# Window attention into a mixture of attention experts: fp16 pairs scaled by the largest v, stage 1 in two head pairs in step, and a new order of all engines

## The chip, the cores and the metric

The kernel runs on one core of one Trainium2 chip. The metric is the device time of one execution in microseconds, and the median of several runs stands for a kernel. The core's engines are TensorE (PE, with PEld its weight loads), VectorE (DVE), ScalarE (ACT), GpSimd (POOL) and SyncE (SP), which here issues the DMAs.

## The reference

Two stages for 8 batches of 576 positions. Stage 1 is attention over a window of 64 positions, in 8 heads of 64 columns. Its result, 512 columns wide, is x of stage 2: four experts, each full causal attention with its own projections, of which every position takes the two with the largest gate.

```python
scores = scale * np.matmul(q, k.transpose(0, 1, 3, 2))       # stage 1, B 8, H 8, S 576, D 64
mask = (rel >= 0) & (rel < 64)
attn = softmax(np.where(mask, scores, -1e9)); x = attn @ v    # heads side by side: (B, S, 512)

logits = x @ w_gate                                           # stage 2, E 4, Hd 64
w = softmax(two largest logits)
for e in range(E):
    q, k, v = x @ wq[e], x @ wk[e], x @ wv[e]
    a = softmax(causal(scale * q @ k.T))
    ye = a @ v @ wo[e]
    out += (w of e where e is among the two) * ye
```

All inputs and outputs are float32.

## The kernel before

Every engine's instruction order is written out by hand in one long string, ORDER: each word names a unit (a Python generator, made at the end of the kernel), a colon gives it PSUM banks (eight banks of 512 float32 columns), and each time it stands there one step of it is issued. A step's instructions go to whichever engines they belong to, and each engine keeps that order. So the order is static, and a wait on one engine holds all that is queued behind it there.

Stage 1 works on head pairs p (two heads h over 64 partitions each; 4 pairs a batch) and 64-row query blocks b. A group g is four (pair, block) tiles, 9 groups a batch, 72 in all.
- p and h load q, k and v (v in windows of 128 rows for each block, so each row comes twice): `load_pair`, `load_v`, on SP's queue, L211 to L232.
- m computes scores (`s1_mm`, L344) with float32 64x64 quarters of the array, two groups at a time; q is the softmax (`s1_qk`). The first 18 groups (FIRST) keep 128 key columns and go by L364 and L371, and are normalised on GpSimd tile by tile (L420). From group 18 the two key halves of a block, which the window makes complementary, are folded into 64 columns (L380), with L385 to L404 and L422 after them.
- t transposes (`s1_t`, L437 for the first 18 groups, L444 later); from group 18 four VectorE multiplications by the masks tri (L458), each over 64 partitions, unfold the halves and move them between partition halves.
- a multiplies with v over 128 window rows (`s1_av`, L471), takes the largest absolute value (L482), and leaves PSUM as a float32 pair: XH rounded for TensorE (L484) and XL the rest (L486). b gathers the last 64 rows of two batches.

Stage 2 has two expert pairs pr for each batch.
- l and w load and split the weights (`load_weight`, `split_weights`) into pairs in float32 form; `bound` holds a bound from the largest weight.
- n and N (`s2_top`, `s2_scale`, L585) work out the scales SC of a batch from the largest x and that bound.
- v, k and r project (`s2_v`, `s2_k`, `s2_q`), each product as three matmuls of high and low parts (`three`, L573 to L575); results go to fp16 pairs, scaled by SC. Keys' halves are 320 and 256 columns.
- x and y are scores (`s2_mm`, L703, L709) and softmax (`s2_soft`, L721, L725), u splits the weights of attention into fp16 high and low parts (`s2_w`, L767 to L778), D transposes them by DMA (`s2_turn`, L786, issued on SP), A multiplies with v (`s2_av`, L819), o is the output projection (`s2_o`, L573 to L575 with 512 columns, L847 out of PSUM, L850 to DRAM).
- g is the gate (`s2_gate`).

There is one set of the large tiles P2, PX, SPLIT and TURN for both expert pairs. For the last batch IDLE puts matmuls of no use (L810) between those of `s2_av`, 47 in all.

Of the kernel before, what the change touches and what calls it, by code (L numbers as in the profile page):

```python
# [28 lines left out]
FIRST = 18  # L29
SOLO = 2  # L30
ECOPY = (0, 1, 0, 0, 0, 1, 0, 1, 0, 0, 0, 0, 0, 0, 0, 0, 0, 0)
# [3 lines left out]
IDLE = {(7, 0, 1): (12, 6), (7, 1, 1): (5, 24)}  # L35
# [929 lines left out]
```

## Time and profile before

| | us |
|---|---|
| median of 3 runs | 440.78 (440.49 to 441.65) |
| profiled execution, its span | 442.2 |
| TensorE busy | 418.8 (95%) |
| VectorE busy | 379.5 (86%) |
| ScalarE busy | 342.1 (77%) |
| GpSimd busy | 302.8 (68%) |
| DMA | 81.74 MB in 142778 packets |

Busy time is the share in which an instruction of the engine is under way. A matmul's record holds its way through the array, so matmuls overlap in the records; the distance from one start to the next is what one costs in a run of them. PEclk is the granted clock of TensorE: 1.00 is 2.4 GHz, 0.5 is 1.2 GHz, and values between are means over a stretch. The chain that ended last is followed back from the last instruction, at each step to what released it.

### The profile page before, as it was taken

Reading aid. Unit: us, or ns where it says so; the run is one execution under the profiler, and the core shown is the slowest. Engines: PE = TensorE matmul, PEld = TensorE weight load, DVE = VectorE, ACT = ScalarE, POOL = GpSimd, SP = SyncE. Lnnn points to the kernel's source line nnn. Section 1 sums busy time; section 2 is a strip of 40 time slices with the busy share of each in tenths; the row PEclk is TensorE's granted clock in tenths of the full one; section 3 lists DMA queues with packets and bytes.
Section 4 is the critical chain, followed back from the end, with each engine's and each line's share of the span. In section 5 each row is a group of like instructions: output and inputs, shape, how many; then the busy total and the mean of one; then the engine's idle time right before and its main releaser. Section 6 shows DMA issues by size and latency. Waiting matters only on the chain. (4 is left out here: it accounts for less than half of the span.)

```text
span 442.2 us, 15325 instructions
## 1 busy us (share of the span) xinstructions
PE 418.8 (95%) x5655; PEld 360.8 (82%) x5655; DVE 379.5 (86%) x1254; ACT 342.1 (77%) x1174; POOL 302.8 (68%) x697
## 2 busy tenths in 40 slices
PE   7889999999999999999899988999999999999876
PEld 6669798987889889797788778988889888888655
DVE  3798898999999999899799996999997998788811
ACT  4977899877887878798578794968788867789722
POOL 6767779788696877978578974588866885722200
PEclk9899999999999999999899998999999999999989
DMA  8962266876799799679868999758997596659992
GB/s 263 386 206 114 66 216 137 199 180 167 161 175 248 166 207 235 148 210 196 196 156 185 178 243 195 178 129 231 230 211 195 111 215 120 130 100 207 206 201 95
DMA packets 142778, 81.74 MB, mean 185 GB/s; under 512 B 124656, under 2 KB 125680, under 8 KB 142704
## 3 DMA queue, kind: packets, MB, share of 16 engines
q1 hardware_dynamic: 142624, 80.64, 79.0%
q8 instruction: 44, 0.72, 0.7%
q14 instruction: 30, 0.25, 0.2%
q10 hardware_dynamic: 80, 0.13, 0.1%
HBM read 40.90 MB, written 9.44 MB: 114 GB/s over the span
## 5 line engine op out<-in xcount | busy, mean ns | idle before, releaser
L778 POOL TENSOR_TENSOR sp<-p,sp 128x320 f16<-128x320 f32 (+3 forms) x110 | 101.0, 919 | 9.2
L725 ACT ACTIVATE p<-p,r 128x192 f32<-128x192 f32 (+3 forms) x128 | 77.5, 611 | 14.6 <-DVE r L721 14.6
L777 POOL TENSOR_SCALAR p<-p,r 128x320 f32<-128x320 f32 (+3 forms) x110 | 64.6, 587 | 22.0 <-ACT sp L767 17.9
L767 ACT ACTIVATE sp<-p,r 128x448 f16<-128x448 f32 (+3 forms) x128 | 73.8, 615 | 4.6 <-POOL r L759 2.9
L458 DVE TENSOR_TENSOR pt<-ps,tri 64x512 f32<-64x512 f32 (+1 forms) x120 | 75.3, 633 | 1.8
L721 DVE CUSTOM_DVE_ANT_0 p<-ps,causal,sc 128x320 f32<-128x320 f32 (+2 forms) x128 | 63.7, 544 | 0.9 <-PE ps L703 0.3
L819 PE MATMUL ps<-tu,v 128*64 128x64 f16 (+2 forms) x1056 | 42.1, 233 | 5.1 <-DMA tu<-sp 3.8
L471 PE MATMUL ps<-pt,v 128*64 128x64 f32 x1080 | 41.9, 235 | 4.6 <-DMA v<-in_vW_dram 3.2
L819 PEld LDWEIGHTS <-v 128*64 128x64 f16 x1056 | 38.6, 114 | 9.1 <-issue 7.5
L471 PEld LDWEIGHTS ps<-pt,v 128*64 128x64 f32 x1080 | 37.2, 147 | 10.0 <-DVE ps L380 2.7
L344 PE MATMUL ps<-k,q 64*64 64x128 f32 (+1 forms) x1080 | 40.1, 271 | 4.2 <-DMA k<-in_kT_dram 3.8
L391 ACT ACTIVATE p<-ps,st 128x64 f32<-128x64 f32 x144 | 43.2, 318 | 1.1 <-POOL st L387 1.1
L703 PE MATMUL ps<-kt,qt 64*128 64x320 f16 (+3 forms) x480 | 40.3, 292 | 0.6 <-DVE m L721 0.3
L573 PE MATMUL ps<-xh,wkhi 128*128 128x320 f32 (+1 forms) x128 | 39.5, 309 | 0.0
L573 PE MATMUL ps<-xh,wqhi 128*128 128x256 f32 (+1 forms) x128 | 39.2, 306 | 0.0
L344 PEld LDWEIGHTS ps<-k,q 64*64 64x64 f32 x1080 | 31.1, 133 | 9.2 <-issue 4.9
L575 PE MATMUL ps<-xh,wklo 128*128 128x320 f32 (+1 forms) x128 | 37.9, 296 | 0.0
L575 PE MATMUL ps<-xh,wqlo 128*128 128x256 f32 (+1 forms) x128 | 37.8, 296 | 0.0
L574 PE MATMUL ps<-xl,wkhi 128*128 128x320 f32 (+1 forms) x128 | 37.8, 295 | 0.0
L574 PE MATMUL ps<-xl,wqhi 128*128 128x256 f32 (+1 forms) x128 | 37.7, 295 | 0.0
L573 PE MATMUL ps<-wvhi,xh 128*128 128x260 f32 x128 | 37.4, 292 | 0.1
L574 PE MATMUL ps<-wvlo,xh 128*128 128x260 f32 x128 | 36.3, 284 | 0.9 <-DVE wvlo L308 0.9
(158 smaller groups left out, 1224.1 us busy)
## 6 DMA issues: line engine op xcount, KB each, us to landing
v<-in_vW_dram SPq DMA_DIRECT2D x30, 576.0 KB, 5.1
k<-in_kT_dram SPq DMA_DIRECT2D x29, 320.0 KB, 4.0
q<-in_qT_dram SPq DMA_DIRECT2D x29, 288.0 KB, 3.5
out_dram<-out SPq DMA_DIRECT2D x32, 256.0 KB, 3.0
tu<-sp SPq DMA_TRANSPOSE x96, 4.3
out_dram<-out SPq DMA_DIRECT2D x7, 128.0 KB, 3.4
sp<-in_kT_dram SPq DMA_DIRECT2D x2, 320.0 KB, 5.9
p<-in_qT_dram SPq DMA_DIRECT2D x2, 288.0 KB, 5.6
```

Of the source, the lines that this page charges most:

```text
L344: nc.tensor.matmul(S1[g][i][o:o + 64, c:], lhsT=q_t[r, 64 * b:64 * b + 64], rhs=k_t[r, 64 * b + c:64 * b + 128], start=True, stop=True)
L458: nc.vector.tensor_mul(t[64 * w:64 * w + 64, :n, e], ps[r, :n], tri[r, w, None, :].to_broadcast([64, n, 128]))
L471: nc.tensor.matmul(o[64 * h:64 * h + 64, 4 * x + i], lhsT=pairs[p][2][:, h, b], rhs=t[:, i, c:c + 64], start=True, stop=True)
L573: nc.tensor.matmul(ps, lhsT=ah, rhs=bh, start=first, stop=False)
L574: nc.tensor.matmul(ps, lhsT=ah, rhs=bl, start=False, stop=False)
L575: nc.tensor.matmul(ps, lhsT=al, rhs=bh, start=False, stop=last)
L721: nc.vector.tensor_tensor_reduce(out=dst, in0=src, in1=mask, scale=SC[b][:, 6:7], scalar=above, op0=OP.add, op1=OP.min, accum_out=to)
L725: nc.scalar.activation(p, p, AF.Exp, bias=r2[:, 0, x:x + 1], scale=-1.0, accum_out=r2[:, 1, x:x + 1])
L767: nc.scalar.activation(hi, p, AF.Copy, scale=by)
L777: nc.gpsimd.tensor_scalar(p, p, by, 1.0, op0=OP.mult, op1=OP.mult)
L778: nc.gpsimd.tensor_tensor(lo, p, hi, op=OP.subtract)
L819: nc.tensor.matmul(to, lhsT=V2[b % 2][:, c, a, 2 * pr + h], rhs=rhs, start=n == 0, stop=n == len(work_list) - 1, skip_group_check=True)
```

## The change

What it does:
- x, the four weights and y become fp16 pairs, not float32 pairs. The three products of each stay. The scale of x is the largest absolute v of its batch (`s1_top`, `s1_scale`: two reductions over the loaded v, a transposition on TensorE, a reduction, and a product with ones that spreads the number), as a weighted mean of v can't exceed it. The scale of each weight matrix comes from its column sums (`split_weights`: absolute values on ScalarE, 14 bf16 products with a constant, a reduction). `s2_scale` has only two or three small GpSimd instructions left.
- Stage 1 has one form for all groups, the folded one. A tile group is two blocks of a double pair d (two head pairs e, each with two heads h): a group's four tiles are two blocks by two e. In batch 0 the groups alternate between its two d, so that all heads of a block are done together (`rows`). Groups 0 to 3, 8 and the last go alone in `s1_mm`, the others by two.
- v is loaded once (one load per d, 16 in all, and a small one for the rows before), in three buffers. `s1_t` has one multiplication over 128 partitions, which leaves each e in its half; `s1_av` then contracts over 64 partitions, in four quarters of the array (e by h), into two banks. Adjacent blocks that share v go in one matmul of 128 columns.
- P2, PX, SPLIT, TURN and KT exist twice, one for each expert pair; the 64-row block of the scores is a unit of its own (k == 4) with its own bank.
- The low parts of batch 0's k and q are made on GpSimd, by a copy from ScalarE. For the last expert pairs (LATE) the high parts of three blocks are made on GpSimd.
- IDLE goes. The last three transpositions go to TensorE (BY_PE: fp16 products with the identity, in halves, and copies to SBUF by ScalarE and VectorE). The outputs of the last batch from j = 2 are made in halves on two queues.
- ORDER is new from end to end. It has 31 filler products (`keep_busy`, words that begin with F), all in the start.

The core of the diff (ORDER and what repeats a pattern left out):

```diff
-FIRST = 18
-SOLO = 2
...
-IDLE = {(7, 0, 1): (12, 6), (7, 1, 1): (5, 24)}
+BY_PE = ((7, 1, 1, 1), (7, 1, 2, 0), (7, 1, 2, 1))
...
+    def load_v(d):
+        v_t = values[d]
+        rows = vW.rearrange("d r c -> (d r) c")[256 * d + 64:256 * d + 192].rearrange("r (h b c) -> r h b c", h=2, b=BLK)
+        nc.sync.dma_start(v_t[:, :, 0:BLK], rows)
...
     def split_weights(i):
...
+        nc.scalar.activation(size, raw, AF.Abs)
+        yield
...
+        for x in range(c):
+            nc.tensor.matmul(ps, lhsT=above_one, rhs=size[:, x], start=x == 0, stop=x == c - 1)
+        yield
...
-        hi = const.tile([128, n], F32R, name=f"w{name}hi")
-        lo = const.tile([128, n], F32R, name=f"w{name}lo")
+        hi = const.tile([128, n], F16, name=f"w{name}hi")
+        lo = const.tile([128, n], F16, name=f"w{name}lo")
...
     def s1_t(g):
...
-            for e in range(2):
-                r = slice(64 * e, 64 * e + 64)
-                for w in range(2):
-                    nc.vector.tensor_mul(t[64 * w:64 * w + 64, :n, e], ps[r, :n],
-                                         tri[r, w, None, :].to_broadcast([64, n, 128]))
-                    yield
+        nc.vector.tensor_tensor(t, ps[:, :, None].to_broadcast([128, n, 2, 128]),
+                                tri[:, None].to_broadcast([128, n, 2, 128]), op=OP.mult)

     def s1_av(g):
...
+            nc.tensor.matmul(to, lhsT=values[d][r, h, b + e - (w == 0)], rhs=rhs, start=(e, h) not in started,
+                             stop=s == n - 1, skip_group_check=True)
...
+        by = SC[b9][:, 0:1]
+        nc.scalar.activation(hi, src, AF.Copy, scale=by)
+        yield
+        nc.vector.scalar_tensor_tensor(lo, src, by, hi, op0=OP.mult, op1=OP.subtract)
         yield
...
+    def s1_top(b):
+        MV[b] = work.tile([128, 3], F32, tag="mv", name=f"mv_{b}")
+        for x in range(2):
+            nc.vector.tensor_reduce(MV[b][:, x:x + 1], values[2 * b + x].rearrange("r h b c -> r (h b c)"),
+                                    axis=AX.X, op=OP.max, apply_absolute_value=True)
+            yield
+        nc.vector.tensor_tensor(MV[b][:, 2:3], MV[b][:, 0:1], MV[b][:, 1:2], op=OP.max)
+
+    def s1_scale(b):
+        ps = bank()
+        nc.tensor.transpose(ps[0:1, 0:128], MV[b][:, 2:3], ident)
+        yield
+        m = work.tile([1, 1], F32, tag="m1", name=f"m1_{b}")
+        nc.vector.tensor_reduce(m, ps[0:1, 0:128], axis=AX.X, op=OP.max)
+        yield
+        nc.tensor.matmul(ps[:, 256:257], lhsT=one, rhs=m, start=True, stop=True)
+        yield
...
     def s2_turn(b, pr, k, low):
...
+        if (b, pr, k, low) not in BY_PE:
+            nc.sync.dma_start_transpose(dst.rearrange("r (a c) -> r a c", a=n), src)
+            return
+        parts = []
+        for half in range(2):
+            c = slice(64 * n * half, 64 * n * half + 64 * n)
+            ps = bank().bitcast(F16)[:, :64 * n]
+            for a in range(n // 2):
+                nc.tensor.transpose(ps[:, 128 * a:128 * a + 128], src[:, c][:, 128 * a:128 * a + 128], ident_h)
+            parts.append((dst[:, c], ps))
+            yield
+        copy(*parts[0])
+        yield
+        copy(*parts[1], vector=True)
...
-            for _ in range(idle[low] if n in (0, 2 * len(AVS[part])) else 0):
...
-    Y8 = [[const.tile([128, 2, 512], F32R, name=f"y{b}{i}") for i in range(2)] for b in range(2)]
+    Y8 = [[const.tile([128, 2, 512], F16, name=f"y{b}{i}") for i in range(2)] for b in range(2)]
...
     def s2_o(b, j):
-        ends = (b, j) == (NB - 1, 4)
+        ends = b == NB - 1 and j > 1
...
+    def keep_busy(n, of):
+        ps = bank()[:, :128]
+        for _ in range(n):
+            nc.tensor.matmul(ps, lhsT=of, rhs=of, start=True, stop=True)
```

## Rows read from the trace of the kernel before

**Rows 1.** The page's first section: busy time of each engine, its share, instructions.

```profile
span 442.2 us, 15325 instructions
PE 418.8 (95%) x5655; PEld 360.8 (82%) x5655; DVE 379.5 (86%) x1254; ACT 342.1 (77%) x1174; POOL 302.8 (68%) x697
```

**Rows 2.** Windows: us, busy PE, PEld, DVE, ACT, POOL, clock, DMA share, GB/s.

```profile
0.00:31.20 31.20, 26.31 (x426) 20.61 (x427) 20.92 (x115) 22.45 (x91) 23.66 (x82) 0.95 0.79 279
31.20:414.00 382.80, 372.06 (x5042) 323.31 (x5038) 350.96 (x1124) 309.93 (x1062) 276.78 (x614) 0.99 0.80 178
212.00:222.00 10.00, 7.99 (x134) 7.15 (x133) 6.86 (x17) 4.90 (x15) 5.69 (x11) 0.83 0.77 172
262.00:272.00 10.00, 7.49 (x157) 6.75 (x157) 6.48 (x16) 4.73 (x11) 6.39 (x11) 0.83 0.73 203
414.00:442.20 28.20, 20.47 (x193) 16.88 (x191) 7.65 (x18) 9.71 (x23) 2.38 (x3) 0.92 0.74 168
```

**Rows 3.** Waits of TensorE: who waited, for whom, total, times, longest.

```profile
PE ps L344 <- DMA k<-in_kT_dram: 3.8, 3, 2.0
PE ps L819 <- DMA tu<-sp: 3.8, 3, 3.1
PE ps L471 <- DMA v<-in_vW_dram: 3.2, 3, 2.5
```

**Rows 4.** Timeline of TensorE (start, duration, instruction): projections, output products, output products late.

```profile
209.80 0.28 PE L575 MATMUL ps<-xh,wklo 128*128 128x256 f32 x1
209.92 0.29 PE L573 MATMUL ps<-xh,wkhi 128*128 128x256 f32 x1
...
207.14 0.39 PE L574 MATMUL ps<-wolo,y 128*128 128x512 f32 x1
207.37 0.39 PE L575 MATMUL ps<-wohi,y 128*128 128x512 f32 x1
...
424.51 0.63 PE L574 MATMUL ps<-wolo,y 128*128 128x512 f32 x1
424.94 0.63 PE L575 MATMUL ps<-wohi,y 128*128 128x512 f32 x1
```

**Rows 5.** The chain that ended last, in order of time (start, length, what).

```profile
418.17 5.48 DMA tu<-sp
...
430.23 2.40 PE ps L810 x22
```

**Rows 6.** Timeline of TensorE: products of stage 1, scores, scale products, transpositions.

```profile
204.94 1.15 PE L471 MATMUL ps<-pt,v 128*64 128x64 f32 x32
...
202.97 1.16 PE L344 MATMUL ps<-k,q 64*64 64x128 f32 x32
...
222.05 0.72 PE L585 MATMUL ps<-top,bound 128*128 128x1 f32 x6
222.70 1.09 PE L344 MATMUL ps<-k,q 64*64 64x128 f32 x32
224.55 0.63 PE L444 MATMUL ps<-ident,p 128*128 128x128 f32 x4
```

**Rows 7.** Groups by line and shape: busy us, mean ns of one, idle before.

```profile
L471 PE MATMUL ps<-pt,v 128*64 128x64 f32 x1080 | 41.9, 235 | 4.6 <-DMA v<-in_vW_dram 3.2 <-ACT pt L199 0.8 <-DVE p L400 0.6
L458 DVE TENSOR_TENSOR pt<-ps,tri 64x512 f32<-64x512 f32 x96 | 65.8, 686 | 1.5
L458 DVE TENSOR_TENSOR pt<-ps,tri 64x256 f32<-64x256 f32 x24 | 10.1, 419 | 0.3
L482 DVE TENSOR_REDUCE mx<-ps 128x1 f32<-128x512 f32 x32 | 21.7, 680 | 6.8 <-PE ps L471 6.7
L482 DVE TENSOR_REDUCE mx<-ps 128x1 f32<-128x256 f32 x8 | 3.2, 404 | 0.0
```

**Rows 8.** Timeline of TensorE in the start: first product with v, first projection.

```profile
17.60 3.30 PE L471 MATMUL ps<-pt,v 128*64 128x64 f32 x64 [0.78 <-ACT pt L199]
...
31.20 0.39 PE L573 MATMUL ps<-wvhi,xh 128*128 128x260 f32 x1
```

More of the change, by code (lines that the diff above doesn't have):

```diff
@@ L226, in load_v @@
-    def load_v(p):
-        if p in EARLY:
-            v_t = EARLY[p][2].rearrange("r (h b c) -> r h b c", h=2, b=BLK)
-        else:
-            v_t = load.tile([128, 2, BLK, 64], F32, tag="v", name=f"v{p}")
-        nc.sync.dma_start(v_t, vW[p].rearrange("r (h b c) -> r h b c", h=2, b=BLK))
-        pairs[p][2] = v_t
+    P2 = [[const.tile([128, 1024 * (part + 1)], F32, name=f"p2_{s}{part}") for part in range(2)] for s in range(2)]
+    PX = [const.tile([128, 2, 64], F32, name=f"px{s}") for s in range(2)]
@@ new lines, in window_attention_moe_attention, with rows, score_set @@
+    XT = {}
+    def rows(g):
+        for x in range(2):
+            y = 2 * (g % 9) + x
+            if g < 8:
+                yield g % 2, g - g % 2 + x
+            elif g == 8:
+                yield x, 8
+            else:
+                yield 2 * (g // 9) + y // BLK, y % BLK
+    def score_set(g):
+        if g in (8, NG1 - 1):
+            return (g,)
+        first = g - (g + (g > 8)) % 2
+        return first, first + 1
+    def s1_mm(gs):
+        for g in gs:
+            S1[g] = bank().rearrange("r (t c) -> r t c", c=128)
@@ L336, in s1_mm @@
         for i in range(4):
             for g in gs:
-                p, b = list(tiles(g))[i][1:]
-                c = 64 if i in alone(g) else 0
-                q_t, k_t, _ = pairs[p]
+                d, b = list(rows(g))[i // 2]
+                c = 0 if b else 64
+                q_t, k_t = pairs[d]
                 for h in range(2):
                     r = slice(64 * h, 64 * h + 64)
-                    o = 64 * (h ^ turn(g, i))
-                    nc.tensor.matmul(S1[g][i][o:o + 64, c:], lhsT=q_t[r, 64 * b:64 * b + 64],
-                                     rhs=k_t[r, 64 * b + c:64 * b + 128], start=True, stop=True)
@@ L347, in turn @@
-    def turn(g, i):
-        return i % 2 if g < SOLO else g % 2
+                    o = 64 * (h ^ g % 2)
+                    nc.tensor.matmul(S1[g][o:o + 64, i, c:], lhsT=q_t[r, i % 2, 64 * b:64 * b + 64],
+                                     rhs=k_t[r, i % 2, 64 * b + c - 64:64 * b + 64], start=True, stop=True)
     def s1_qk(g):
         ps = S1.pop(g)
-        lone = alone(g)
-        z = 4 if g % 2 and g >= FIRST else 0
-        def sums():
-            if z == 0:
-                ST[g] = work.tile([128, 3, 8], F32, tag="st1", bufs=4, name=f"st1_{g}")
-            return ST[g - z // 4]
-        if g < FIRST:
-            st = sums()
-            pt = P1[g] = work.tile([128, 4, 128], F32, tag="sm1", bufs=4, name=f"sm1_{g}")
-            for i, p, b in tiles(g):
-                nc.vector.tensor_tensor_reduce(out=pt[:, i], in0=ps[i], in1=win[:, int(b == 0)], scale=-0.125,
-                                               scalar=3.0e38, op0=OP.add, op1=OP.min,
-                                               accum_out=st[:, 0, z + i:z + i + 1])
-                if i == 1:
-                    yield
+        both = score_set(g)
@@ new lines, in s1_qk @@
+        z = 4 * both.index(g)
+        old, own = ps[:, :, 0:64], ps[:, :, 64:128]
+        first = [b == 0 for _, b in rows(g)]
+        if any(first):
+            for x in range(2):
+                c = slice(2 * x, 2 * x + 2)
+                nc.vector.copy_predicated(own[:, c], past[:, None].to_broadcast([128, 2, 64]),
+                                          win[:, None].to_broadcast([128, 2, 64]) if first[x] else old[:, c])
+        else:
+            nc.vector.copy_predicated(own, past[:, None].to_broadcast([128, 4, 64]), old)
@@ L464, in s1_av @@
         gs = members(g)
-        o = bank().rearrange("r (t c) -> r t c", c=64)
-        for x, y in enumerate(gs):
-            t = PT1.pop(y)
-            for i, p, b in tiles(y):
-                for h in range(2):
-                    c = 64 * (h ^ turn(y, i))
-                    nc.tensor.matmul(o[64 * h:64 * h + 64, 4 * x + i], lhsT=pairs[p][2][:, h, b],
-                                     rhs=t[:, i, c:c + 64], start=True, stop=True)
-        yield
-        if b9 not in XH:
-            XH[b9] = work.tile([128, NP * S], F32R, tag="xh", name=f"xh{b9}")
-            XL[b9] = work.tile([128, NP * S], F32R, tag="xl", name=f"xl{b9}")
@@ new lines, in s1_av, with product @@
+        o = [bank() for e in range(2)]
+        started = set()
+        def product(e, h, s, w, wide):
+            r = slice(64 * e, 64 * e + 64)
+            d, b, c = slots[s]
+            c ^= 64 * h
+            rhs = t[r, s, w, c:c + 64]
+            to = o[e][64 * h:64 * h + 64, 64 * s:64 * s + 64]
+            if wide:
+                rhs = bass.AP(rhs.tensor, rhs.offset, [rhs.ap[0], [128 + (slots[s + 1][2] ^ 64 * h) - c, 2], [1, 64]])
+                to = o[e][64 * h:64 * h + 64, 64 * s:64 * s + 128].rearrange("r (a c) -> r a c", a=2)
+            nc.tensor.matmul(to, lhsT=values[d][r, h, b + e - (w == 0)], rhs=rhs, start=(e, h) not in started,
+                             stop=s == n - 1, skip_group_check=True)
+            started.add((e, h))
@@ new lines, in s1_av @@
+        quarters = [(e, h) for e in range(2) for h in range(2)]
+        for s in range(n):
+            if slots[s][1] and (s == 0 or slots[s - 1][0] != slots[s][0]):
+                for e, h in quarters:
+                    product(e, h, s, 0, False)
+            wide = s + 1 < n and slots[s + 1][0] == slots[s][0]
+            for e, h in quarters:
+                product(e, h, s, 1, wide)
+        yield
+        src = o[0][:, :64 * n]
+        two = [src.ap[0], [512 * (at[1] - at[0]), 2]]
@@ L674, in s2_k @@
         yield
-        if (b, pr) not in KT:
-            KT[b, pr] = work.tile([128, 2, S], F16, tag="kt", name=f"kt_{b}_{pr}")
-        yield from parts(ps, KT[b, pr][:, :, c0:c0 + n], SC[b][:, 4:5])
-    def parts(ps, t, by):
-        nc.scalar.activation(t[:, 0], ps, AF.Copy, scale=by)
-        yield
-        nc.vector.scalar_tensor_tensor(t[:, 1], ps, by, t[:, 0], op0=OP.mult, op1=OP.subtract)
+        yield from parts(b, half, ps, *(KT[pr][:, x, c0:c0 + n] for x in range(2)))
     def s2_q(b, pr, half):
@@ L686, in s2_q @@
         yield
-        yield from parts(ps, QT[pr][:, :, c0:c0 + n], SC[b][:, 5:6])
+        yield from parts(b, 2 + half, ps, *(QT[pr][:, x, c0:c0 + n] for x in range(2)))
     SCORES = (((1, 0, 192), (2, 0, 320)), ((3, 0, 448),), ((4, 0, 320),), ((4, 320, 256),))
@@ L696, in s2_mm @@
     def s2_mm(b, pr, k):
+        if k == 4:
+            ps = SB[b, pr, k] = bank()
+            for x, (w, m) in enumerate(((0, 0), (0, 1), (1, 0))):
+                for e in range(2):
+                    r = slice(64 * e, 64 * e + 64)
+                    nc.tensor.matmul(ps[r, 0:64], lhsT=QT[pr][r, w, 0:64], rhs=KT[pr][r, m, 0:64],
+                                     start=x == 0, stop=x == 2)
+            return
         ps = SB[b, pr, k] = [bank() for e in range(2)]
@@ L842, in s2_o @@
         for h, (c, ps) in enumerate(done):
[L843 removed]
+            by = SC[b][:, 2:3] if j < 4 else SC4[b][:, 0:1]
             if h:
@@ L849, in s2_o @@
         if j < 4:
-            nc.sync.dma_start(out[b, 128 * j:128 * j + 128], t)
+            for h, (c, _) in enumerate(done):
+                (nc.scalar if h else nc.sync).dma_start(out[b, 128 * j:128 * j + 128, c], t[:, c])
+                yield
         else:
```

416 lines of the change are left out of this document (204 added, 212 removed), and 232 rows, old and new, of the table ORDER.

## The prediction

> **What bounds the kernel now.** I read the page's first section first [rows 1]. TensorE shows work for 95% of the span, VectorE for 86%, ScalarE for 77%, GpSimd for 68%. A busy share is modelled from pipelined matmuls, so I then cut the span into stages [rows 2]. From 31.2 to 414 us (the middle) TensorE stands still for 10.7 of 382.8 us, and nearly half of that lies in two short stretches, 212 to 222 and 262 to 272 us, where the granted clock is 0.83: a wait, and then a stretch at half clock. The reader should see that everywhere else in the middle no other engine is as full: TensorE bounds it, and its time falls only if its own instructions become fewer or cheaper. Two stages differ. Before 31.2 us no projection has started: TensorE stands 4.9 us and much of the rest is waiting between small pieces. After 414 us TensorE has 20.5 us of work in 28.2 us, and VectorE, ScalarE and GpSimd are nearly empty: this is a chain, not a load. The waits of TensorE name the rest [rows 3]: the landing of k, of v and of a transposition.
>
> The profiled execution spans 442.2 us, 1.4 us above the median of the runs (440.78). I make the sum against 442.2 and take off 1.4 at the end.
>
> **Projections in fp16 pairs (s2_v, proj, s2_o): -15.6 us.** The number of products stays: 432 for v (32 groups of 12 and 4 pairs of last blocks of 12), 768 for k and q (64 groups of 12), 222 for the output (37 of 6), 1422 in all. What changes is the price of one. With f32 operands, a matmul of 256 columns starts 120 ns after the one before, and one of 512 columns 230 ns after [rows 4]. The trace has one fp16 form with 128 rows and 256 columns that stands in an unbroken run: 22 in 2.40 us, 109 ns each [rows 5]. So fp16 saves 11 ns at 256 columns; the step from 256 to 512 costs 110 ns, which is 256 columns at 2.4 GHz and little more, so the 11 ns are a fixed part that I take at every width. 1422 x 11 ns = 15.6 us, all of it on the bounding engine. The bounds: 0, since the fp16 form has a stationary side of 64 columns and a 128-wide one may be held back by its weight load, and 15.6; I take the upper end, because the row is nearest in columns and rows.
>
> The Trainium skill (TensorE: Matmul & The Clock Gate, Back-to-back issue gap) has a warm bf16 matmul of N columns start N/2.4 + 2.5 ns after the one before; the 109 ns agree, and by it 512 columns would take 216 ns, a saving of 14 ns there and 0.7 us more in the sum.
>
> **Transpositions of stage 1 (s1_t): -3.9 us.** The first 18 groups transposed four 128x128 pieces each, the new form two: 36 fewer at about 109 ns (four in 0.63 us with a last one that shows its latency) [rows 6].
>
> **Products of stage 1 (s1_av): +3 us.** Per batch there were 72 matmuls over 128 rows; there are now 88 over 64 rows in four quarters of the array, 48 of 128 columns and 40 of 64. An instruction of the old kind costs 1.15 us/32 = 36 ns; one over quarters with 128 columns (the scores, L344) costs 1.16 us/32, the same [rows 6]. If the narrow ones cost half, this is 68 against 72 (-6% of 41.9 us, the group's busy time [rows 7], -2.3 us); if they cost as much, +22% (+9.3 us). I take +3, between, as weight loads of 64 columns stay the same. The scores themselves stay, except that six groups now go alone and use half of the array, about 0.5 us each; four of them lie in the start, where TensorE waits, so I cost them at nothing, and at 3 us if that cover goes.
>
> **Scales: -0.1 us.** The six products per batch with bound (48 at 108 ns [rows 6], 5.1 us) give way to a transposition and a one-column product, four instructions of that price, 3.5 us. Column sums of the weights add 14 matmuls, 1.5 us by the 109 ns. So nothing on load; the waits that they bring are a rival, below. The 31 filler products in the start are 62 instructions, 6.8 us at 109 ns against 22 before; they stand where TensorE waits for v and for the scale, so I cost the surplus (4.4 us) at nothing.
>
> **VectorE, ScalarE, GpSimd: nothing directly.** The masking after the transposition was four instructions over 64 rows (96 of 686 ns and 24 of 419 ns, 75.9 us) [rows 7] and is one over 128 rows: by the step of 267 ns for 256 columns 1024 cost 1.22 us, and 32 x 1.22 + 8 x 0.69 = 44.5 us. VectorE sheds 31 us here. The maximum over v replaces that over the attention's result: 16 of 1280 columns, some 1.5 us each, 24 us, against 32 of 680 ns and eight halves, 25 us [rows 7]. VectorE falls to about 345 us, under TensorE by 50. ScalarE gains the absolute weights and the batch 0 copies and loses 15 copies; GpSimd loses the normalisation in 128-column pieces. None is the bound, so this buys slack for the order, and no sum.
>
> **The middle's waits: -4 us.** v is loaded once per two heads' pairs instead of doubled in windows: half of 32 loads of 576 KB go, 9.4 of 81.74 MB, and there are three v buffers instead of two. The waits for k and v are 3.8 and 3.2 us, and the two stretches at half clock each cost 10 x (1 - 0.83) = 1.7 us: 10.4 us together [rows 2, 3]. Bounds 0 and -10.4; I take under half, because a new order moves all loads.
>
> **The start: -3 us.** The first product with v starts at 17.6 us, the first projection at 31.2 [rows 8]. In the new order v of the first two loads comes right after q and k, two head pairs go in step, so that a query block of all heads is complete after few groups, and projections of it may start earlier. Against that the result can't leave PSUM until the maximum of v is known (two reductions of 1.5 us, a transposition, a reduction, a product, a reciprocal: some 4 us after v lands). Bounds +4 (all of that on the path) and -10; I take -3.
>
> **The tail: -8 us.** The chain of waits shows a DMA transposition of 5.48 us [rows 5], for which TensorE waits 3.1 us [rows 3], then output products at 0.43 us instead of 0.23, the clock at half [rows 4, 5], then 22 filler products, 2.40 us. The last three transpositions go to TensorE: 28 of 128 columns and six copies out of PSUM, of which the last ten and two copies lie in the chain, some 2.5 us (10 x 109 ns and two copies of 0.69 [rows 7]). So -3, -1.7 for the clock, -2.4 for the fillers, -1 for the last outputs in halves: -8. Bounds: -2, if the two pairs in step leave more work behind the last softmax, and -12. What is late next is the exponentials of the last pair, and then the five output tiles.
>
> **Sum:** -15.6 - 3.9 + 3 - 0.1 - 4 - 3 - 8 = -31.6; 442.2 - 31.6 - 1.4 = 409.2 us.
>
> **Rivals.**
> (B) Only the load goes. The order is rewritten whole; waits that leave come back elsewhere, as start, middle and tail together are worth 15 of the 31.6 us. Then 442.2 - 16.6 - 1.4 = 424 us. For it: the DMA engines stay at 0.7 to 0.9 of their time in every stage [rows 2]. Against: VectorE's slack.
> (C) fp16 is no cheaper with a 128-column stationary side, so that the change doesn't do on TensorE what its types promise: 409.2 + 15.6 = 425 us.
> (D) The tail stays at half clock. The fillers after the last softmax go, and what comes in their place is transpositions. After the wait of 3.1 us the clock fell to 1.2 GHz and each of the 512-column products took 0.20 us more [rows 2, 4, 5]. With 30 such products and some 1 us of attention products behind the last transposition, 7 us more: 416 us. The Trainium skill (TensorE: Matmul & The Clock Gate, Part 4) says that a transposition on TensorE doesn't count as busy for the clock as a matmul does; by it this rival is what happens, but no row here shows a stretch of transpositions alone.
> (E) All waits go and the start takes its full gain: about 398 us.
> (F) Slower. The scale puts two waiting instructions per batch into TensorE's queue: the transposition waits for the maximum over v, which waits for v's landing, and the one-column product waits for VectorE again. All matmuls queue behind them. A wait of that kind costs 2.5 us and 1.7 us of half clock, 4.2 us, as at 262 us [rows 2, 3]. It turns the sum at 31.6/4.2, some eight such waits; at two in each of eight batches the time is 409 + 67 = 476 us. Against it: the scale is needed only when the products leave PSUM, and the units stand far from their neighbours in the order (n1 and M1 lie tens of units apart).
>
> **How the numbers follow.** Forecast (402 to 417) 0.47, B 0.21, C 0.10, D 0.10, E 0.06, F 0.06. The predicted time is the forecast's, 409. The range leaves out F and half of E and the far side of B and C: 398 to 426. A measurement of this kernel can tell about 0.3% from no change, 1.3 us. Faster holds all but F and the few cases in which B and F meet: 0.92; same 0.02; slower 0.06.
>
> **What would show it.** In the changed profile: fp16 projection matmuls of 256 columns 109 ns apart (120: C); TensorE's busy time near 397 us; masking in 40 instructions near 1.2 us; VectorE near 345 us; first projection before 28 us; no stretch of the middle with a clock under 1 (the waits at M units: F); from the last exponential to the end under 20 us and the last output products 0.23 us or less (0.43: D). The prediction is wrong if a group of products of stage 1 costs over 1.5 us, or if TensorE's idle time in the middle grows.

## The result, and the profile after

The kernel after takes 419.61 us (median of 4 runs, 416.86 to 421.06), the kernel before beside it 441.02 (440.49 to 441.65): a ratio of 0.951 [0.948, 0.955]. It is faster by 21.4 us where 31.6 were forecast; 419.6 lies inside the range, 10.4 us above the predicted 409.2. Some executions of a kernel fall into a slower state; the medians and ratios in this document are of the others.

The first section of the page after (span; busy us, share, instructions of each engine):

```profile
span 418.5 us, 15632 instructions
PE 389.9 (93%) x5943; PEld 295.9 (71%) x5944; DVE 337.9 (81%) x1044; ACT 333.1 (80%) x1150; POOL 300.9 (72%) x682
```

Beside [rows 1] TensorE lost 28.9 us of work and VectorE 41.6, and the span lost only 23.7. Where they went shows best by two landmarks that both kernels have: the first projection and the end of the last exponential. The last exponential of the kernel before, from the timeline of ScalarE:

```profile
414.71 0.77 ACT L725 ACTIVATE p<-p,r 128x576 f32<-128x576 f32 x1
```

Windows of the kernel before between the landmarks, middle and tail (us, busy PE, PEld, DVE, ACT, POOL, clock, DMA share, GB/s):

```profile
31.20:415.48 384.28, 373.54 (x5056) 324.58 (x5054) 352.44 (x1125) 311.41 (x1065) 278.18 (x616) 0.99 0.81 179
415.48:442.20 26.72, 18.99 (x182) 15.60 (x177) 6.17 (x16) 8.23 (x20) 0.98 (x1) 0.92 0.73 162
```

The landmarks of the kernel after, from its timeline (the first projection and the last exponential):

```profile
25.14 0.27 PE L580 MATMUL ps<-wvhi,xh 128*128 128x260 f16 x1
...
395.16 0.76 ACT L720 ACTIVATE p<-p,r 128x576 f32<-128x576 f32 x1
```

And its windows, middle and tail:

```profile
25.14:395.92 370.78, 353.13 (x5483) 265.98 (x5483) 311.82 (x972) 307.58 (x1076) 282.21 (x614) 0.99 0.77 163
395.92:418.50 22.58, 15.13 (x188) 10.54 (x186) 9.58 (x22) 10.67 (x24) 3.81 (x7) 1.00 0.72 158
```

The start went from 31.2 to 25.1 us (-6.1), the middle from 384.3 to 370.8 (-13.5), the tail from 26.7 to 22.6 (-4.1). In the middle the first busy column, TensorE, fell by 20.4 us, but the time in which it stands still rose from 384.3 - 373.5 = 10.7 to 370.8 - 353.1 = 17.7 us. A second profiled execution of the kernel after, taken later, has a middle of 367.0 us and 15.5 us of standing still in it:

```profile
24.76:391.78 367.02, 351.51 (x5483) 265.00 (x5483) 311.50 (x972) 307.69 (x1076) 283.43 (x614) 0.99 0.76 165
```

So single executions of one kernel differ by some 4 us in the middle, and the rise is 5 to 7 us. It is the finding of this case: the load went, and waiting took a quarter to a third of it back.

What TensorE waits for has changed sides. The view of its waits, after (who <- for whom: us, times, longest):

```profile
PE ps L403 <- DVE pt L406: 2.3, 3, 1.7
PE ps L795 <- ACT sp L767: 1.8, 1, 1.8
PE ps L705 <- DVE kt L671: 1.4, 1, 1.4
PE ps L403 <- DVE xl L455: 1.4, 1, 1.4
PE ps L403 <- DVE p L372: 1.3, 1, 1.3
PE ps L827 <- DMA tu<-sp: 1.2, 2, 1.0
...
PE ps L337 <- DMA k<-in_kT_dram: 0.5, 1, 0.5
```

Adding up all rows of that view: before, 18.3 us of waits, of which DMAs release 11.3 and VectorE 3.8; after, 23.4 us, of which DMAs release 1.7 and VectorE 17.0. In the middle alone VectorE's part went from 2.7 to 13.3 us and that of the DMAs from 5.9 to 0.7. The three large waits of [rows 3] (k, a transposition, v) are gone or small. In their place stand 36 short ones, most of them for something that VectorE was still to do. No single one is worth more than 1.8 us.

The prices of the single pieces, after. Timeline of TensorE (start, duration, instruction): keys at 256 columns, outputs at 512:

```profile
387.72 0.27 PE L581 MATMUL ps<-xl,wkhi 128*128 128x256 f16 x1
387.83 0.27 PE L582 MATMUL ps<-xh,wklo 128*128 128x256 f16 x1
...
383.06 0.38 PE L581 MATMUL ps<-wolo,y 128*128 128x512 f16 x1
383.27 0.38 PE L582 MATMUL ps<-wohi,y 128*128 128x512 f16 x1
383.49 0.38 PE L580 MATMUL ps<-wohi,y 128*128 128x512 f16 x1
```

Groups after (count | busy us, mean ns of one | idle before, releaser): masks, reductions over v, products with v:

```profile
L406 DVE TENSOR_TENSOR pt<-ps,tri 128x1024 f32<-128x1024 f32 x32 | 38.9, 1214 | 1.9 <-PE ps L428 1.9
L406 DVE TENSOR_TENSOR pt<-ps,tri 128x512 f32<-128x512 f32 x8 | 5.4, 677 | 0.3 <-PE ps L403 0.3
L471 DVE TENSOR_REDUCE mv<-vt 128x1 f32<-128x1280 f32 x16 | 23.7, 1484 | 14.0 <-DMA vt<-in_vW_dram 14.0
L428 PE MATMUL ps<-pt,vt 64*64 64x64 f32 (+1 forms) x1440 | 40.8, 257 | 2.1 <-DVE xl L455 1.1
```

An fp16 product of 256 columns starts 0.11 us after the one before, one of 512 columns 0.21 to 0.22 us; in [rows 4] it was 0.12 and 0.23.

### The profile page after: what moved, and what is told of

It is laid out like the page before. It is cut to its first block, busy times and chain, and to the rows that moved or that the text cites. A ratio compares the mean times of both kernels' runs of the same rounds, so it can differ in the third digit from the quotient of the medians.

```text
span 418.5 us, 15632 instructions
## 1 busy us (share of the span) xinstructions
PE 389.9 (93%) x5943; PEld 295.9 (71%) x5944; DVE 337.9 (81%) x1044; ACT 333.1 (80%) x1150; POOL 300.9 (72%) x682
## 4 chain that ended last, share of the span: by engine, by line
PE 50%; DVE 19%; DMA 15%; POOL 6%; issue 5%; ACT 3%; SPq 1%; POOLq 0%; ACTq 0%; DVEq 0%
DMA vt<-in_vW_dram 9%; PE ps L580 8%; PE ps L581 7%; PE ps L582 7%; PE ps L337 6%; PE ps L827 6%; PE ps L705 5%; PE ps L428 5%; DVE p L716 4%; DMA tu<-sp 3%; PE ps L403 3%; DVE pt L406 3%; DVE mv L471 2%; POOL sp L778 2%; DMA out_dram<-out 1%
## 5 line engine op out<-in xcount | busy, mean ns | idle before, releaser
L778 POOL TENSOR_TENSOR sp<-p,sp 128x192 f16<-128x192 f32 (+3 forms) x110 | 100.7, 915 | 9.2
L720 ACT ACTIVATE p<-p,r 128x448 f32<-128x448 f32 (+3 forms) x128 | 77.4, 609 | 7.5 <-DVE r L716 7.3
L777 POOL TENSOR_SCALAR p<-p,r 128x192 f32<-128x192 f32 (+3 forms) x110 | 65.0, 591 | 6.3 <-ACT sp L767 4.8
L390 POOL TENSOR_TENSOR p<-p,st 128x256 f32<-128x256 f32 x72 | 43.1, 614 | 10.5 <-DVE st L386 8.2
L406 DVE TENSOR_TENSOR pt<-ps,tri 128x1024 f32<-128x1024 f32 (+1 forms) x40 | 44.3, 1107 | 2.2 <-PE ps L428 1.9
L365 ACT ACTIVATION_READ_ACCUMULATOR p<-ps,st 128x1 f32 x204 | 43.2, 212 | 0.0
L428 PE MATMUL ps<-pt,vt 64*64 64x64 f32 (+1 forms) x1440 | 40.8, 257 | 2.1 <-DVE xl L455 1.1
L581 PE MATMUL ps<-xl,wkhi 128*128 128x320 f16 (+1 forms) x128 | 36.8, 287 | 1.0 <-DVE xl L455 1.0
L580 PE MATMUL ps<-xh,wkhi 128*128 128x320 f16 (+1 forms) x128 | 36.8, 288 | 0.1
L582 PE MATMUL ps<-xh,wklo 128*128 128x320 f16 (+1 forms) x128 | 36.8, 287 | 0.0
L582 PE MATMUL ps<-xh,wqlo 128*128 128x256 f16 (+1 forms) x128 | 36.6, 286 | 0.0
```

The source lines that it names most:

```text
L365: nc.scalar.activation(pt[:, i], ps[:, i, 64:128], AF.Exp, bias=st[:, 0, z + i:z + i + 1], scale=0.125, accum_out=st[:, 1, z + i:z + i + 1])
L428: nc.tensor.matmul(to, lhsT=values[d][r, h, b + e - (w == 0)], rhs=rhs, start=(e, h) not in started, stop=s == n - 1, skip_group_check=True)
L580: nc.tensor.matmul(ps, lhsT=ah, rhs=bh, start=first, stop=False)
L581: nc.tensor.matmul(ps, lhsT=ah, rhs=bl, start=False, stop=False)
L582: nc.tensor.matmul(ps, lhsT=al, rhs=bh, start=False, stop=last)
L720: nc.scalar.activation(p, p, AF.Exp, bias=r2[:, 0, x:x + 1], scale=-1.0, accum_out=r2[:, 1, x:x + 1])
```

## The experiments

Two theories stood against each other. T: TensorE bounds the middle, so that its load falls through to the time, and what is missing is one new wait, for which the reductions over v were suspected: VectorE stands 14.0 us before them until v has landed (third line above). R, rival B widened: the middle is bounded by TensorE and VectorE together through a fixed order, so that a load which leaves one of them comes back as a wait for the other. Every ratio is against the kernel before, run on the same chip.

**One part alone, in the order of before: fp16.**

```diff
-F32R = mybir.dt.float32r
+F32R = mybir.dt.float16
...
-            nc.scalar.activation(yh, src, AF.Copy)
+            nc.scalar.activation(yh, src, AF.Copy, scale=1.0 / UP)
```

> The kernel before with its old order, where x, the four weights and y are fp16 pairs instead of float32 pairs (one type name, and y scaled down as it leaves PSUM so that it fits; the weights are not scaled, so small ones lose digits). Theory (the projections are load on the bounding engine): products of 256 columns 109 ns apart, of 512 columns 216, and 1422 x 11 to 15 ns = 16 to 17 us come off the whole: 424 to 426 us. Rival (the order is fixed and its other engines are close, so a lighter TensorE only waits more): TensorE's busy time falls by 16 us or more and its idle time rises by at least half of that; 432 us or more.

Measured: 439.25 us against 440.77, 0.996 [0.991, 1.001]. The first section of its page:

```profile
PE 404.1 (92%) x5655; PEld 301.1 (69%) x5655; DVE 377.9 (86%) x1254; ACT 340.5 (78%) x1174; POOL 302.2 (69%) x697
```

Its windows between the landmarks:

```profile
31.27:415.30 384.03, 361.04 (x5061) 269.68 (x5058) 351.14 (x1125) 309.80 (x1065) 277.47 (x615) 0.99 0.83 179
415.30:438.70 23.40, 16.51 (x178) 10.80 (x173) 5.71 (x15) 8.22 (x19) 0.96 (x2) 0.98 0.81 178
```

TensorE's busy time fell by 14.7 us, as the price says. The middle stayed at 384.0 us: its idle time rose from 10.7 to 23.0. By the sum over its waits the DMAs' share is as before (11.6 us against 11.3) and VectorE's went from 3.8 to 12.4. So this step's price was nearly right (15.6 us had been forecast) and its place on the path was wrong: the time lies where the rival had it (432 us or more), not at 424 to 426.

**One part alone: masking in one instruction.** Groups 18 to 71 of the kernel before:

```diff
-            for e in range(2):
-                r = slice(64 * e, 64 * e + 64)
-                for w in range(2):
-                    nc.vector.tensor_mul(t[64 * w:64 * w + 64, :n, e], ps[r, :n],
-                                         tri[r, w, None, :].to_broadcast([64, n, 128]))
-                    yield
+            nc.vector.tensor_tensor(t[:, :n], ps[:, :n, None].to_broadcast([128, n, 2, 128]),
+                                    tri[:, None].to_broadcast([128, n, 2, 128]), op=OP.mult)
```

> The kernel before with the masking of groups 18 to 71 in one multiplication over 128 partitions; the halves stay in their partitions, so that products of stage 1 get masked halves that don't belong to them (that part of the result is not the reference's; all shapes and counts stay). VectorE sheds 43 us, TensorE nothing. By the prediction (TensorE alone bounds the middle): 0.99 to 1.0 of before. If VectorE bounds alone: 0.93 or less. If both bound: 0.97 to 0.99, a little from waits that end earlier.

Measured: 440.18 us against 440.87, 0.997 [0.993, 1.001]. VectorE lost 41.4 us of work (379.5 to 338.1) and the time did not move. That fits T (0.99 to 1.0); the 0.97 to 0.99 of a bound of both engines is missed.

**Both together, in the order of before.**

> The kernel before with both: fp16 pairs as in the run with fp16 alone, and the masking in one multiplication (that part of the result is not the reference's). If TensorE alone bounds, it is the sum of the two alone, about 0.99. If TensorE and VectorE bound together, both must be lighter before the time falls: 0.95 to 0.965, more than the sum of the two alone.

Measured: 434.45 us against 440.87, 0.984 [0.978, 0.990]. The first section of its page:

```profile
PE 401.1 (93%) x5655; PEld 299.6 (69%) x5655; DVE 337.1 (78%) x1164; ACT 341.0 (79%) x1174; POOL 303.0 (70%) x697
```

Its windows between the landmarks:

```profile
30.77:409.20 378.43, 356.68 (x5042) 267.42 (x5038) 310.18 (x1035) 310.50 (x1065) 278.29 (x615) 0.99 0.84 182
409.20:432.90 23.70, 18.20 (x192) 12.29 (x191) 5.95 (x15) 8.13 (x20) 0.81 (x2) 1.00 0.78 174
```

6.4 us, where the two alone give 1.5 and 0.7: only when both engines are relieved does the middle move (384.3 to 378.4), which T does not foresee. It is a narrow finding: the two ratios alone multiply to 0.993, just outside the interval of both together, and have intervals of their own. And 0.984 is nearer to T's sum of about 0.99 than to the 0.95 to 0.965 that R had expected. TensorE still stands for 21.8 us of this middle, and 9.1 us of that is waiting for VectorE, which is at work for only 82% of it now; with fp16 alone, at 91%, it was 10.5 us. So a full VectorE is at most a small part of why TensorE waits for it. The remaining 14 to 15 us to the kernel after (0.984 to 0.951) come with the new order and what it needs: between these profiled executions 5.6 us of start, 7.6 of middle, 1.1 of tail.

**The other way round: the kernel after with masking in four.**

```diff
+        for e in range(2):
+            r = slice(64 * e, 64 * e + 64)
+            for w in range(2):
+                nc.vector.tensor_mul(t[r, :, w], ps[r], tri[r, w, None, :].to_broadcast([64, n, 128]))
```

> The changed kernel where the one masking multiplication over 128 partitions is four over 64 partitions again (the same data into the same places): VectorE gets some 31 us more, 369 us. By the prediction (VectorE is not the bound, its slack is some 50 us): 419 to 423 us. New theory (VectorE bounded the middle together with TensorE, and this edit is what released it): 428 us or more.

Measured: 463.14 us against 440.87, 1.050 [1.043, 1.057]. The first section of its page:

```profile
PE 399.2 (86%) x5944; PEld 302.0 (65%) x5944; DVE 392.2 (85%) x1164; ACT 336.7 (73%) x1150; POOL 302.3 (65%) x682
```

Its largest waits of TensorE:

```profile
PE ps L707 <- DVE pt L409: 9.6, 7, 2.1
PE ps L582 <- DVE pt L409: 6.3, 6, 1.4
PE ps L430 <- DVE pt L409: 5.6, 6, 1.5
PE ps L403 <- DVE pt L409: 5.1, 3, 2.8
```

Its middle, as a window:

```profile
26.90:440.14 413.24, 362.25 (x5484) 271.77 (x5483) 364.72 (x1089) 311.12 (x1077) 283.56 (x614) 0.97 0.68 146
```

VectorE got 54 us more (31 had been expected; all 40 groups of masks are dearer here, where the kernel before had that form in only 30), and the time rose by 43 us. "No sum" for VectorE is refuted in this direction: 0.8 us of time for each us of work. The two longest waits, L707 and L582, are scores and projections of stage 2, which read no mask; only L430 (products with v) does. For the seven waits of scores the order gives the reason: t14:7 and x011:71, t16:6 and x010:61, t19:0 and x003:05, t26:7 and x102:27, t50:7 and x403:76, t52:1 and x412:13, t71:0 and x612:01 are in each case the transposition whose bank a mask reads, and the unit that gets this bank next. So these scores wait for a PSUM bank, and a group's masks hold it for 2.6 us (1.5 in the groups of half size) where the single mask takes 1.2 (0.7). The waits of L582 were not followed in this way. The run therefore does not part two causes: more work on VectorE, and banks that come free later.

**TensorE given its load back.** A product of 80 columns with zeros after each group of three:

```diff
-        nc.tensor.matmul(ps, lhsT=al, rhs=bh, start=False, stop=last)
+        nc.tensor.matmul(ps, lhsT=al, rhs=bh, start=False, stop=False)
+        nc.tensor.matmul(ps[:, :80], lhsT=nought, rhs=bh[:, :80], start=False, stop=last)
```

> The changed kernel with a product of 80 columns with zeros added to each triple of projection products: 474 or more at 33 ns, 16 us more of TensorE, about what fp16 took off; the result doesn't change. If TensorE is on the path everywhere after the change: 434 to 438 us. If TensorE has slack now: under 428 us.

Measured: 429.34 us against 441.59, 0.971 [0.968, 0.975]; the unchanged kernel after, run beside it, 419.79. The first section of its page:

```profile
PE 405.9 (95%) x6421; PEld 315.3 (74%) x6422; DVE 340.3 (80%) x1044; ACT 335.6 (78%) x1150; POOL 302.2 (71%) x683
```

Its middle, as a window:

```profile
25.72:405.70 379.98, 368.05 (x5942) 284.12 (x5942) 314.07 (x972) 310.06 (x1077) 283.38 (x614) 0.99 0.74 160
```

16.0 us of work cost 9.5 us; TensorE's idle time in the middle fell from 17.7 to 11.9. So in the new order TensorE is on the path for about 0.6 of each us (0.5 beside the second execution of the kernel after, where TensorE was busy for 387.9 us). The time lies between the two that were expected. The forecast had 1, the order of before gave (fp16 alone, in the middle) about 0.

**The suspect: the maximum over v.** Three runs. A constant instead of the reductions for batches 1 to 7; reductions of the same size over a tile that is always there; and the true reductions, 5 to 18 places later in ORDER:

```diff
+        if b > 0:
+            yield
+            yield
+            nc.vector.memset(MV[b][:, 2:3], 1.0)
+            return
```

> The changed kernel without the maximum over v for batches 1 to 7: a constant 1.0 stands for it, so VectorE neither reduces (14 of 1.49 us) nor waits there for v to land (14.0 us in the changed profile); the order is the same. Theory (this wait is where the middle's expected gain went): 405 to 412 us, TensorE idle in the middle down from 17.5 us to near 11. Rival (the middle's waits come from the order's other chains, ScalarE's and GpSimd's, and VectorE's stall is absorbed): 416 to 420 us.

```diff
+            still = tri.rearrange("r a c -> r (a c)")[:, None].to_broadcast([128, 5, 256])
+            for x in range(2):
+                nc.vector.tensor_reduce(MV[b][:, x:x + 1], still, axis=AX.XY, op=OP.max, apply_absolute_value=True)
```

> The changed kernel where the reductions of batches 1 to 7 read a tile that has been there since the start instead of v: the same 1280 columns and about the same 1.49 us each, but nothing to wait for; the scale is the constant 1.0. It parts the wait from the load. If the wait costs: near the kernel without the maximum, 406 to 413 us. If VectorE's load costs: near the changed kernel, 417 to 421 us.

```diff
...
-    'q16 y004 q16 m19:54 n1 r010 r010 v03 r010 v02:3 q16 n1 q20 q16 n2 q16 r001:2 v02 g00 k010:6 v03 r001 g00 r001 '
+    'q16 y004 q16 m19:54 r010 r010 v03 r010 v02:3 n1 q16 n1 q20 q16 q16 r001:2 v02 g00 k010:6 v03 r001 g00 r001 v02 '
+    'n2 q19 r001 g00 M1:3 g00 x000:21 k010 M1 k010 t14:7 g00 y000 k010 M1 y000 m17:60 y000 g00 y000 x014:2 M1 p5 '
...
```

> The changed kernel with the reductions over v of batches 1 to 7 some 5 to 18 places later in the order where VectorE stood waiting for v to land (and the scale's steps behind them in batches 4 to 6, with banks that are free there): the same work, other VectorE work ahead of the wait. If the wait is what costs, some 3 us under the changed kernel on this chip (0.7%), as where the reductions read a resident tile; VectorE's wait for v falls from 14 us to under 5. If any change of the order costs as much as it brings: within 0.3% of the changed kernel.

> The changed kernel itself beside the other three, on the same chip: 0.948 to 0.955 of before.

Measured, in that order: 413.99 us against 440.77, 0.940 [0.931, 0.949]; 414.49 against 440.77, 0.943 [0.937, 0.949]; 418.93 against 441.59, 0.949 [0.946, 0.952]; and the unchanged kernel, 419.79 against 441.59, 0.948 [0.944, 0.952]. VectorE's wait for v, in the view of waits of the unchanged kernel run again:

```profile
DVE mv L471 <- DMA vt<-in_vW_dram: 11.1, 11, 3.3
```

The same wait in the kernel with later reductions:

```profile
DVE mv L471 <- DMA vt<-in_vW_dram: 1.7, 2, 1.3
```

The middle of the kernel with later reductions, as a window:

```profile
26.02:395.50 369.48, 352.24 (x5483) 264.90 (x5483) 313.03 (x972) 308.11 (x1077) 283.28 (x614) 0.99 0.79 164
```

With the reductions later the wait is all but gone, and the time is the same; TensorE's waits behind VectorE add up to 17.5 us there, as in the kernel after (17.0). This although the chain of waits put much on that load of v. The chain of the kernel after, by engine and by line (shares of the span), and one of its pieces in order of time:

```profile
PE 50%; DVE 19%; DMA 15%; POOL 6%; issue 5%; ACT 3%; SPq 1%; POOLq 0%; ACTq 0%; DVEq 0%
DMA vt<-in_vW_dram 9%; PE ps L580 8%; PE ps L581 7%; PE ps L582 7%; PE ps L337 6%; PE ps L827 6%; PE ps L705 5%; PE ps L428 5%; DVE p L716 4%; DMA tu<-sp 3%; PE ps L403 3%; DVE pt L406 3%; DVE mv L471 2%; POOL sp L778 2%; DMA out_dram<-out 1%
...
124.98 6.80 DMA vt<-in_vW_dram
```

The chain of the kernel with later reductions, by engine:

```profile
PE 50%; DVE 24%; ACT 10%; POOL 6%; issue 5%; DMA 3%; POOLq 0%; ACTq 0%; DVEq 0%
```

DMA went from 15% to 3%, ScalarE and VectorE took its place: the chain found another way of the same length. The suspect falls as the place of the missing gain. The two runs without the wait lie 0.8 and 0.5% under the unchanged kernel by their ratios, and their intervals overlap its own; their times lie between what the two theories had, and TensorE's idle time in their middles is 13.2 and 14.0 us, not the 11 expected, against 15.5 to 17.7 in the unchanged kernel and 17.2 with later reductions. Some 2 to 4 us for the wait stay possible. And the run that also spares VectorE 18 us of reductions is no faster than the one that keeps them. So 18 us less on VectorE gain nothing in this order, while the 54 us of the masks cost; the masks hold PSUM banks that TensorE needs, and the reductions, which read v, hold none.

**The tail: the last transpositions by DMA again.**

```diff
-BY_PE = ((7, 1, 1, 1), (7, 1, 2, 0), (7, 1, 2, 1))
+BY_PE = ()
```

> The changed kernel where the last three transpositions go by DMA again. By the prediction's term the chain gets 5.5 us for 2.5 us, and the clock may fall in the wait: 422 to 426 us. If the tail is bounded by what runs beside it (output tiles, DMA to memory), 419 to 421 us.

Measured: 423.95 us against 440.77, 0.964 [0.958, 0.971]. Its DMA is issued at the step at which only the first half of the weights is written, so that the second half it moves is old. Issued a step later:

```diff
-        if (b, pr, k, low) not in BY_PE:
+        if (b, pr, k, low) in BY_PE:
+            yield
+        if True:
```

> The changed kernel with the last three transpositions by DMA, each issued where its second half went to TensorE, so that it takes both halves after they are written. By the prediction's term (5.5 us for 2.5 us in the chain, and some clock): 423 to 427 us, 0.96 to 0.968 of before. If the tail is bounded otherwise: 0.951 to 0.955.

Measured: 424.66 us against 440.87, 0.962 [0.957, 0.968]: some 5 us more than the kernel after. Its tail, as a window:

```profile
397.51:423.60 26.09, 15.56 (x160) 10.17 (x158) 8.47 (x19) 9.00 (x21) 3.83 (x7) 0.85 0.83 172
```

TensorE's timeline in it:

```profile
406.94 0.69 PE L829 MATMUL ps<-tu,v 128*64 128x256 f16 x10 [2.89 <-DMA tu<-sp]
407.56 0.61 PE L580 MATMUL ps<-wohi,y 128*128 128x512 f16 x1
407.96 0.63 PE L581 MATMUL ps<-wolo,y 128*128 128x512 f16 x1
```

A wait of 2.89 us, and then products 0.40 us apart at half clock: the pattern of [rows 4, 5], back. The tail is 3.5 us longer than after.

**The fillers of the start left out.**

```diff
-        for _ in range(n):
+        for _ in range(0):
```

> The changed kernel without the 31 filler products of the start. By the prediction (they stand where TensorE waits): 0 to -1 us if the clock holds, and +2 to +4 us if TensorE's clock falls to half in the start, since products wait there some us at a time.

Measured: 420.72 us against 441.59, 0.951 [0.947, 0.955], within 1 us of the unchanged kernel. The window from 0 to 25 us then has a clock of 0.80 (1.00 with them), and the first projection comes at 26.6 instead of 25.1 us. That they cost nothing is confirmed; that they bring anything cannot be told.

## Why the prediction was right, and where it was not

The direction and the range held. The range (398 to 426) also holds B, C and D, so it does not tell the forecast from them, and two errors offset each other in the total: TensorE's work came out 7 us lower than expected, and its idle time in the middle 5 to 7 us higher instead of lower. By the prediction's own signs it is wrong there: "TensorE's idle time in the middle grows" came true. The other sign did not: a group of products of stage 1 takes 1.0 to 1.1 us, not over 1.5.

By stage, between the landmarks, the spans say: start -6.1 (forecast -3), tail -4.1 (-8), middle -13.5 (the rest of the 31.6, -20.6). That leaves 7.9 us. The other 2.5 are the step from span to median: the forecast took 1.4 off the span, since the profiled execution of before lay that much above its median; the span after lies 1.1 below its own median.

**The step that failed** is "all of it on the bounding engine", with its other half, that VectorE's relief "buys slack for the order, and no sum", and the -4 for the middle's waits. Its premise was read from the windows: no other engine is as full [rows 2]. But the engines hand tiles and banks to each other many times in each batch, in an order that is fixed, so a lighter TensorE can come sooner to a wait for VectorE. TensorE's load in the middle fell by 20.4 us, more than the 16.6 that the sum had for the whole kernel, and 7.0 of them (4.8 in the second execution) came back as waiting, where 4 were to be gained. fp16 alone, in the old order, moved the middle by 0.3 us; the lighter masks alone moved the time by 0.3%; both by 1.6%; and in the new order TensorE's work counts for about 0.6. That VectorE was nearly as full (352 of 384 us, 92%) is not shown to be the reason: the waits for it stayed with both parts, at 82%, and 18 us less of its work gained nothing.
The -4 itself was right in its mechanism: the waits for DMAs fell from 11.3 to 1.7 us. It was wrong in its sign, because 13 us of waits for VectorE came in, 10.6 of them in the middle.

Rival B told this best ("waits that leave come back elsewhere", 424 us); the time lies between it and the forecast, nearer to B (4 us against 10). It was named for the right reason and dismissed for the wrong one: VectorE's slack. (E's 398 us do not come out of its bounds: 6.4 us more of waits and 7 more of start off 409.2 give 396. Nothing hangs on it here.)

**The other terms.**
- fp16 pairs: the price was right. TensorE's busy time fell by 14.7 us with fp16 alone, for 15.6. The starts stand 0.11 us apart at 256 columns, and by 383.06, 383.27, 383.49 some 215 ns at 512, where 11 ns taken off [rows 4] gave 219. The Trainium skill (TensorE: Matmul & The Clock Gate, Back-to-back issue gap) has 216 ns for 512 columns, as the gap of an isolated product, and is the better of the two. The same section has 131 ns for a sustained stream of 512-column products; the trace does not show that. Rival C falls.
- Products of stage 1: +3 had the wrong sign. The 1440 records (two for each product, so 90 products a batch and not 88) take 40.8 us of busy time. The 41.9 of [rows 7] are 1080 of the 1152 records of before; with those of batch 0 that read other tiles the whole is 44.4 us, as the window of that line over the span has it, so the term is -3.6, beyond the lower bound of -2.3. The narrow form costs about half, as that bound had it:

```profile
0.00:442.20 442.20, 44.41 (x1152) 39.50 (x1152) 0.98 0.80 185
```

- VectorE near 345 us, masks near 1.2 us: 337.9 us, 1214 ns.
- TensorE near 397 us: 389.9. Of the 7 us less, 6.6 are the products of stage 1.
- Start: the first projection at 25.1 us, "before 28". The gain was twice the term, within its bounds.
- Tail: the transposition was right, the sum too large. Of the -8, the DMA's wait and its clock are worth 3.5 to 5 us by the run with the DMA. But fp16 alone, which changes nothing of the tail's form, has a tail of 23.4 us at a clock of 0.98, and the kernel before with the new masks alone one of 24.2. So of the 26.7 of [rows 2]'s execution, some 2.5 us go with a half clock that other executions of nearly the same tail do not show, and the new form gains only about 1 to 1.5 us more. What is late next is the split of the last softmax, as the timeline of TensorE after has it:

```profile
399.72 0.45 PE L795 MATMUL ps<-ident_h,sp 128*128 128x128 f16 x5 [1.77 <-ACT sp L767]
...
401.57 1.54 PE L795 MATMUL ps<-ident_h,sp 128*128 128x128 f16 x18
...
405.62 0.45 PE L827 MATMUL ps<-tu,v 128*64 128x256 f16 x10 [1.00 <-DMA tu<-sp]
```

  From the last exponential (395.9) to the last of the transpositions (after 403.5) 7.6 us pass, and one DMA transposition still holds TensorE for 1.0 us after that. "Under 20 us" for the tail was wrong by 2.6.
- Rival D falls: the clock of the tail is 1.00 and the output products stand 0.21 to 0.22 us apart. The Trainium skill (TensorE: Matmul & The Clock Gate, Part 4) has it that a transposition on TensorE does not count as busy for the clock in the way a matmul does; here 28 of them, 18 in one record, stand among other products, and no fall of the clock follows. No run shows transpositions alone.
- "No stretch of the middle with a clock under 1" was wrong: there are two, as before (36 to 48 us at 0.86, 110 to 124 at 0.76). But rival F falls: of the scale's transposition and product the view of waits has one wait of 0.6 us. The two stretches as windows:

```profile
36.00:48.00 12.00, 9.87 (x178) 7.23 (x172) 9.38 (x25) 7.71 (x33) 6.58 (x16) 0.86 0.22 84
110.00:124.00 14.00, 11.41 (x212) 8.55 (x208) 11.96 (x36) 11.59 (x42) 10.74 (x19) 0.76 0.73 135
```

  In the second VectorE is at work for 12.0 of 14 us and releases 2.0 of the 2.5 us of TensorE's waits; in the first a mask releases all 2.1. So the waits for VectorE are paid in clock as well.

**What stays open.** That VectorE releases most of TensorE's idle time in the middle (13.3 of 17.7 us) is shown; that its load alone is the reason is not, since 18 us less of reductions gained nothing. Whether it is the time for which VectorE holds PSUM banks was seen only for the scores in the run with masking in four. Which places of the order make TensorE's waits in the kernel after is not settled: they are 36 and none is large. How the 14 to 15 us between the order of before with both parts and the kernel after divide among the order, the second set of tiles for the expert pairs, the single load of v, and the earlier first projection was not separated. fp16 halves the tiles of the pairs, and the second set was added in the same change; a kernel with float32 pairs and two sets was not tried, so whether part of what fp16 is worth is room and not speed stays open too.

## What to carry to other kernels

When the order of all engines is fixed, don't sum what leaves the fullest one: here 14.7 us of its work, taken out in the old order, gave 0.4% of the time, and 16 us put back in the new order cost 9.5. Try a part of the change alone before its price is added up, and ask what the engine comes to wait for next: a result, or a bank that another engine still reads. A long entry in the chain of waits is a place to test, not a price: here 9% of the span lay on one load, and moving its waiters took the wait away and none of the time. And before a stall or a half clock in a tail is booked as a gain, see in a second execution of nearly the same tail whether it is always there.

## What the hardware showed that was not expected

- The same masks cost 1214 ns as one instruction over 128 partitions and 1024 columns, and 4 x 686 = 2744 ns as four over 64 partitions and 512 columns [rows 7]: the elements are the same in number, the time is 2.3 times as long. One mask over 128 partitions and 512 columns takes 677 ns, as much as one over 64 partitions: the time goes with the columns, and half the partitions save nothing.
- After a wait of 2.89 us in the run with the DMA transposition the next output products stood 0.40 to 0.43 us apart for about 3 us; with waits of 1.77, 0.40 and 1.00 us in the same place the kernel after kept a clock of 1.00. The window in the run with the DMA, at 0.59:

```profile
404.00:412.00 8.00, 5.11 (x43) 2.79 (x40) 1.71 (x4) 1.21 (x5) 0.00 (x0) 0.59 1.18 183
```
